# Three pairs of loads become three single loads in a decode block of attention and a bilinear GLU

## The chip, the cores and the metric

The kernel runs on one core of a Trainium2 chip. Its time is the device time of one execution in microseconds (us). Its engines, as the profile names them, are PE (TensorE, with PEld for its weight loads), DVE (VectorE), ACT (ScalarE), POOL (GpSimd) and SP (SyncE, which here issues nearly all transfers). Transfers between the memory of the chip (HBM) and the core's own memory (SBUF) are carried by 16 DMA engines.

## The reference

One token for each of two batch entries goes through a pre-norm attention block with a cache, and then through a bilinear GLU. All data is float32. B = 2, D = 448, 16 heads of 256 values, 8192 cached positions, F = 1792.

```python
q = (x @ wq).reshape(B, Sq, H, Dh).transpose(0, 2, 1, 3)         # x: layernorm of A_x
scores = jnp.einsum("bhqd,bhkd->bhqk", q, k_cache) * (Dh ** -0.5)
p = _softmax(scores, axis=-1)
o = jnp.einsum("bhqk,bhkd->bhqd", p, v_cache)
h = A_x + o.transpose(0, 2, 1, 3).reshape(B, Sq, H * Dh) @ wo

g = jnp.einsum("bsd,df->bsf", _layernorm(h), w_gate)
u = jnp.einsum("bsd,df->bsf", _layernorm(h), w_up)
h2 = h + jnp.einsum("bsf,fd->bsd", g * u, w_down)
```

Each of the 32 pairs of a head and a batch entry, called a query below, has its own 8 MiB of keys and 8 MiB of values. All of the cache is read once: 512 MiB.

## The kernel before

**Tiling.** The 8192 positions of a query are laid out as 128 partitions with 64 positions each; "16 values" or "48 values" below means so many positions on each partition, and 16 of them are 2 MiB. The queries are worked off one after the other (`for n in range(NQ + 1)`, line 550). For a query, VectorE multiplies the keys in place by the query vector and sums over the 256 elements of each position (`scores`, lines 405 to 419). It does this in parts (`score_parts`, line 399): normally 16 values and then 48. Queries 0, 30 and 31, named in `FINE` (line 55), are done in four parts of 16. `top` then takes the largest score, `softmax` the exponentials on ScalarE, and `mix` (line 444) multiplies the probabilities with the values on TensorE: 32 matmuls a query, two positions of each partition in each, 512 columns wide.

**Buffers.** `k_sb` holds 112 values a partition: the keys of even queries lie at values 0 to 63, those of odd ones at 48 to 111, so that two successive queries share 16 values (`OVER`). `v_sb` holds the values of a single query. A load of keys thus waits until VectorE has summed the first 16 values of the query before, and a load of values until `mix` is done with the query before. The values of the last five queries come in pieces, which `LATE` (lines 24 to 30) lists, some of them in parts of the buffers that have come free already.

**Order.** Each engine has a list of its operations in an order written out by hand; the class `Orders` derives the waits from what each operation reads and writes (lines 88 to 113). SP issues all big loads on one queue, in program order, and stops at the first that has to wait. It begins with the weights of the first queries (`d_w0`) and query 0's keys in the pieces of `FIRST` (lines 21 and 262): the last 16 values, the first 16, the middle 32. After that come query 1's keys, query 0's values, query 2's keys, and so on in turn. TensorE runs a loop over the first 27 queries and straight code after that (line 723).

**The end.** The last query's values come in pieces of 16, 32, 8 and 8. `mix` runs over all but the last of them, `open_sums` (line 536) puts the attention result so far and the residual into two accumulators, and `mix` does the last piece. After the values SP loads a last part of `wo`, the gate's weights in two halves, those of "up" in two halves and the down weights in four pieces (lines 605 to 613). The halves divide the columns: F is cut into four groups of 512, 512, 384 and 384 columns, which run on four strips of 32 columns of TensorE; half 0 has the first 256 columns of each group, half 1 the others (256, 256, 128 and 128). `project` (line 618) runs over four row blocks of D, with four matmuls each, one for each group. The operand `xr` is the centred h; its variance is computed by a matmul that stands between the second and the third row block of the gate, and the reciprocal of variance plus epsilon, `rv`, is the scale with which ScalarE copies the gate to `g_sb` (line 675); it does the normalisation of gate and "up" at once. The two halves of "up" follow, each with its product with the gate, two transposes, and then the matmuls of `down` (line 691) as the down weights land.

Of the kernel before, what the change touches and what calls it, by code (L numbers as in the profile page):

```python
# [12 lines left out]
P = 128  # L13
# [3 lines left out]
NJ = SK // P  # L17
HC = 16
OVER = HC

FIRST = ((NJ - HC, NJ), (0, HC), (HC, NJ - HC))


LATE = (
# [1 line left out]
    ((48, None), (16, None)),  # L26
    ((32, None), (32, None)),
    ((32, None), (32, ("k", 0))),
    ((16, ("k", 32)), (32, ("v", 32)), (8, ("v", 0)), (8, ("v", 8))),
)  # L30
WQ, WO = 3 * 2 * DH + DH, 2 * D

FG = (512, 512, 384, 384)
FO = (0, 512, 1024, 1408)
# [1 line left out]
NG = FG[0] // P  # L36

FH = FG[0] // 2
WIDE = [[min(n, (k + 1) * FH) - k * FH for n in FG] for k in range(2)]
PACKED = [3 * sum(n) + n[0] + n[2] for n in WIDE]  # L40

FF = [(n, g) for n in range(4) for g in range(4) if n < FG[g] // P]

# [7 lines left out]
NQ = H * B  # L51
EARLY = NQ - len(LATE)
LOOP = EARLY
DOWN = (5, 5, 3, 1)
FINE = (0, NQ - 2, NQ - 1)


class Orders:
# [135 lines left out]
def decode_block(nc, x, k_cache, v_cache, w, wg, wu, wd, out):  # L194
# [3 lines left out]
    def sb(name, *shape):  # L198
        return nc.alloc_sbuf_tensor(name, list(shape), F32)[:]
# [15 lines left out]
    def mm(out, lhsT, rhs, start, stop, r=(), w=(), mark=None, **kw):  # L215
        put("PE", "matmul", out, lhsT, rhs, start=start, stop=stop, r=r, w=w, mark=mark, **kw)
# [26 lines left out]
    def load_k(i, lo=0, hi=NJ):  # L243
        load_keys(f"d_k_{i}_{lo}", k_cache, i, lo, hi, "k", k_base(i) + lo)
# [13 lines left out]
    def load_w(name, hp, lo, hi, event=None):  # L258
        o.load("SP", name, w_sb[:, lo:hi], w[hp][:, lo:hi], writes=[("w", lo, hi)], event=event)

    load_w("d_w0", 0, 0, WQ)
    for lo, hi in FIRST:
        load_k(0, lo, hi)
# [80 lines left out]
    def q_at(hp, b):  # L344
        k = hp % 2 * B + b
        return qs[k], f"q{k}"

    for k in range(2):
        for b in range(B):
            for c in range(DC):  # L350
                at = c * 2 * DH + (k * DH if c < DC - 1 else 0)
# [5 lines left out]
            got, name = q_at(0, b)  # L357
# [41 lines left out]
    def score_parts(i):  # L399
        at = [(k - 1) % (NJ // HC) * HC if i % 2 == 0 else k * HC for k in range(NJ // HC)]  # L400
        if i in FINE:
            return [(lo, lo + HC) for lo in at]
# [147 lines left out]
    for n in range(NQ + 1):  # L550
        hp, at = divmod(n, 2 * B)
# [49 lines left out]
    k_flat = k_sb.rearrange("p j d -> p (j d)")  # L601
    places = {"wd": 0, "wg": (NJ - OVER) * DH, "wu": (NJ - OVER) * DH + NF * D}
    wd_t, wg_t, wu_t = (k_flat[:, places[n] :][:, : NF * D] for n in ("wd", "wg", "wu"))
    halves = (slice(0, PACKED[0]), slice(PACKED[0], sum(PACKED)))
    for name, t, src in (("wg", wg_t, wg), ("wu", wu_t, wu)):
        for k, half in enumerate(halves):
            o.load("SP", f"d_{name}_{k}", t[:, half], src[:, half],
                   writes=[("k", places[name] + half.start, places[name] + half.stop)])
    at = 0
# [6 lines left out]
        dve("memset", t[2 * 32 :, wide - (FG[0] - FG[2]) : wide], 0.0, w=[name])  # L616

    def project(out, out_name, t, name, k, between=None):
        wide, t = WIDE[k], t[:, halves[k]]
        here = ("k", places[name] + halves[k].start, places[name] + halves[k].stop)  # L620
        for c in range(DC):
            for g in range(4):
                xs = xr[:, c]
                if c < DC - 1:
                    at = c * sum(wide) + sum(wide[:g])
                else:
                    xs = xr[:, c + g % 2]
                    at = 3 * sum(wide) + (wide[0] if g >= 2 else 0)
                mm(
                    out[32 * g : 32 * g + 32, : wide[g]], xs.rearrange("p b r -> p (b r)"),  # L630
                    t[:, at : at + wide[g]], c == 0, c == DC - 1, r=["xr", here], w=[out_name],
                    mark="PE" if c == DC - 1 and g == 3 else None,
                )
            if c == 1 and between is not None:
                between()

    g_ps = q_ps[0]
# [23 lines left out]
        w=["sr"])  # L661
    var = sm[1][:, :1]
    project(
        g_ps[:, :FH], "q_ps0", wg_t, "wg", 0,
        lambda: mm(var, sr.rearrange("p g b r -> p (g b r)"), avg[:, 0:1], True, True,
                   r=["sr", "avg"], w=["sm1"], mark="PE"),
    )
    project(g_ps[:, FH:], "q_ps0", wg_t, "wg", 1)
    oTs = sb("oTs", P, 2, B, 16)
    dve("tensor_copy", oTs, oT[:, :, :, None].to_broadcast([P, 2, B, 16]), r=["oT"], w=["oTs"])  # L670
    last_head(y_ps, "y_ps", oTs.rearrange("p c b r -> p c (b r)"), "oTs", group, False)
# [19 lines left out]
    def down(lo, hi):  # L691
        for k in range(lo, hi):
            n, g = FF[k]
            for q in range(YN):
# [5 lines left out]
                )  # L700

    project(u_ps[0], "q_ps1", wu_t, "wu", 0)
    blank(u_ps[1], "q_ps0", FH)
    project(u_ps[1], "q_ps0", wu_t, "wu", 1, lambda: product(0))
# [36 lines left out]
def pack(np, inputs):  # L741

    got = {n: np.ascontiguousarray(inputs[n]) for n in ("A_x", "A_k_cache", "A_v_cache")}
    wq, wo = np.asarray(inputs["A_wq"]), np.asarray(inputs["A_wo"])
    n = 2 * DH
    rows = []
    for hp in range(H // 2):
        a = wq[:, hp * n : (hp + 1) * n]
        top = a[: 3 * P].reshape(3, P, n).transpose(1, 0, 2).reshape(P, 3 * n)
        last = np.concatenate([a[3 * P :, :DH], a[3 * P :, DH:]], axis=0)  # L750
        rows.append(np.concatenate([top, last], axis=1))

    wo = wo.reshape(H // 2, 2, 2, P, D).transpose(0, 3, 1, 2, 4).reshape(H // 2, P, 2 * WO)
    none = np.zeros_like(wo[:1]), np.zeros_like(rows[0])
    got["w"] = np.concatenate([np.stack(rows + [none[1]]), np.concatenate([none[0], wo])], axis=2)
    for name in ("B_w_gate", "B_w_up"):
        a = np.asarray(inputs[name])
        rows = []
        for k in range(2):
            col = [a[:, FO[g] + k * FH :][:, : WIDE[k][g]] for g in range(4)]  # L760
            top = np.concatenate(col, axis=1)[: 3 * P].reshape(3, P, sum(WIDE[k])).transpose(1, 0, 2)
            last = [np.concatenate([col[q][3 * P :], col[q + 2][3 * P :]], axis=1) for q in range(2)]
            rows += [top.reshape(P, 3 * sum(WIDE[k])), np.concatenate(last, axis=0)]
        got[name] = np.concatenate(rows, axis=1)
    a = np.asarray(inputs["B_w_down"]).reshape(NF, P, D)
    a = a[[FO[g] // P + n for n, g in FF]]
    got["wd"] = a.transpose(1, 0, 2).reshape(P, NF * D)
    return {k: np.ascontiguousarray(v) for k, v in got.items()}
# [27 lines left out]
```

## Time and profile before

| | us |
|---|---|
| median of 3 runs | 1305.08 (1305.04 to 1305.36) |
| the profiled execution | 1305.22 |
| its span, from the first to the last instruction | 1303.9 |
| VectorE busy | 1131.4 (87% of the span) |
| TensorE busy | 489.9 (38%) |
| ScalarE busy | 62.6 (5%) |
| moved by DMA | 561.35 MB, at a mean of 431 GB/s |

Times within the profile count from the start of the span. In rows of the timeline and of the chain, the first number is the start and the second the duration in us; a row ends, in square brackets, with the idle time of the engine ahead of it and what ended it. In rows of DMA issues the last number is the us from the issue to the landing of all of the load; some rows show no size. The row "DMA" of the page cuts the span into 40 equal parts and gives the busy share of the 16 DMA engines in tenths. All operations are recorded by one helper, hence line L207 in nearly all rows, and L154 for the loads; the tiles tell them apart. A float32 matmul shows in the rows as two records.

### The profile page before, as it was taken

Reading aid. Unit: us, or ns where it says so; the run is one execution under the profiler, and the core shown is the slowest. Engines: PE = TensorE matmul, PEld = TensorE weight load, DVE = VectorE, ACT = ScalarE, POOL = GpSimd, SP = SyncE. Lnnn points to the kernel's source line nnn. Section 1 sums busy time; section 2 is a strip of 40 time slices with the busy share of each in tenths; the row PEclk is TensorE's granted clock in tenths of the full one; section 3 lists DMA queues with packets and bytes.
Section 4 is the critical chain, followed back from the end, with each engine's and each line's share of the span. In section 5 each row is a group of like instructions: output and inputs, shape, how many; then the busy total and the mean of one; then the engine's idle time right before and its main releaser. Section 6 shows DMA issues by size and latency. Waiting matters only on the chain.

```text
span 1303.9 us, 6965 instructions
## 1 busy us (share of the span) xinstructions
PE 489.9 (38%) x3004; PEld 170.2 (13%) x3004; DVE 1131.4 (87%) x280; ACT 62.6 (5%) x184; POOL 1.2 (0%) x8
## 2 busy tenths in 40 slices
PE   3035332263321634306343253333424335243267
PEld 2012100020100201102101021100211011011013
DVE  7997998878988789987889878889788897899981
ACT  1000000000000000000000000000000000000000
POOL 0000000000000000000000000000000000000000
PEclk8567655676655867657666576765766667666588
DMA  9999999999999999999999999999999999999998
GB/s 413 436 424 449 420 448 420 440 422 446 420 447 420 442 422 446 422 440 434 432 426 442 438 424 440 426 423 438 450 418 448 414 448 420 447 421 430 434 422 364
DMA packets 13132, 561.35 MB, mean 431 GB/s; under 512 B 1470, under 2 KB 1600, under 8 KB 2112
## 3 DMA queue, kind: packets, MB, share of 16 engines
q1 hardware_dynamic: 13116, 561.19, 99.7%
q8 instruction: 7, 0.11, 0.0%
q14 instruction: 5, 0.04, 0.0%
q10 hardware_dynamic: 4, 0.00, 0.0%
HBM read 561.19 MB, written 0.00 MB: 430 GB/s over the span
## 4 chain that ended last, share of the span: by engine, by line
DMA 71%; DVE 28%; PE 0%; issue 0%; SPq 0%; POOL 0%; ACT 0%; POOLq 0%; DVEq 0%
DMA k_sb<-in_A_k_cache_dram 68%; DVE k_sb L207 14%; DVE s L207 14%; DMA k_sb<-in_wd_dram 3%; DVE nm L207 0%; PE q_ps L207 0%; PE sm L207 0%; DVE xb L207 0%; PE y_ps L207 0%; DVE o_ps L207 0%; SPq L154 0%; POOL ident L207 0%; DVE m L207 0%; ACT q L207 0%; DVE sum_sq_x L207 0%
## 5 line engine op out<-in xcount | busy, mean ns | idle before, releaser
L207 DVE TENSOR_TENSOR k_sb<-k_sb,q 128x4096 f32<-128x4096 f32 x70 | 556.4, 7949 | 134.0 <-DMA k_sb<-in_A_k_cache_dram 130.4
L207 DVE TENSOR_REDUCE s<-k_sb 128x16 f32<-128x4096 f32 x70 | 556.1, 7945 | 0.3
L207 PE MATMUL o_ps<-v_sb,p 128*2 128x512 f32 x2000 | 290.1, 743 | 398.7 <-PEq L161 375.3
L207 PEld LDWEIGHTS o_ps<-v_sb,p 128*2 128x2 f32 x2000 | 53.7, 97 | 606.0 <-issue 578.9
L207 PE MATMUL sm<-nm,row 1*128 1x1 f32 x64 | 16.6, 326 | 194.0 <-PEq L161 170.6
L207 PE MATMUL sm<-ident,m 128*1 128x128 f32 x32 | 10.5, 329 | 139.1 <-PEq L161 99.5
L207 PE MATMUL q_ps<-w_sb,xb 128*128 128x256 f32 (+1 forms) x172 | 60.4, 510 | 0.0
L207 ACT ACTIVATE o_sb<-o_ps 128x512 f32<-128x512 f32 x32 | 19.1, 597 | 689.6 <-PE o_ps L207 689.6
L207 PE MATMUL sm<-sel,o_sb 128*128 128x1 f32 x256 | 33.7, 253 | 25.7 <-PEq L161 22.1
L207 PEld LDWEIGHTS sm<-nm,row 1*128 1x128 f32 x64 | 14.7, 284 | 203.3 <-issue 178.4
L207 PE MATMUL acc_ps<-w_sb,oT 128*2 128x448 f32 x60 | 36.4, 746 | 12.4 <-PEq L161 11.7
L207 PEld LDWEIGHTS sm<-sel,o_sb 128*128 128x128 f32 x256 | 31.8, 195 | 56.4 <-issue 46.5
L207 PEld LDWEIGHTS q_ps<-w_sb,xb 128*128 128x128 f32 x172 | 34.4, 204 | 31.0 <-issue 28.3
L207 PE MATMUL sm<-lsum,ones 128*128 128x1 f32 x64 | 17.3, 339 | 26.0 <-PEq L161 22.3
L207 ACT ACTIVATE nb<-sm 128x1 f32<-128x1 f32 x32 | 5.5, 171 | 411.7 <-PE sm L207 411.7
L207 PEld LDWEIGHTS sm<-ident,m 128*1 128x1 f32 x32 | 2.6, 80 | 150.5 <-issue 107.8
L207 PEld LDWEIGHTS sm<-lsum,ones 128*128 128x128 f32 x64 | 15.3, 298 | 28.0 <-issue 23.9
L207 ACT ACTIVATE q<-q_ps,rstd 128x512 f32<-128x512 f32 (+1 forms) x18 | 11.5, 639 | 73.1 <-PE q_ps L207 73.1
L207 DVE TENSOR_REDUCE total<-o_ps 128x1 f32<-128x128 f32 x1 | 0.3, 291 | 14.1 <-PE o_ps L207 14.1
L207 ACT ACTIVATE p<-s,nb 128x64 f32<-128x64 f32 x32 | 11.1, 348 | 1.0
L207 ACT ACTIVATE oT<-sm,rl 128x2 f32<-128x2 f32 x32 | 8.4, 262 | 39.1 <-PE sm L207 39.1
L207 PE MATMUL q_ps<-k_sb,xr 128*32 128x256 f32 (+1 forms) x128 | 9.9, 425 | 0.9 <-DVE xr L207 0.7
(81 smaller groups left out, 79.0 us busy)
## 6 DMA issues: line engine op xcount, KB each, us to landing
v_sb<-in_A_v_cache_dram SPq DMA_DIRECT2D x4, 4096.0 KB, 30.6
w_sb<-in_w_dram SPq DMA_DIRECT2D x7, 1792.0 KB, 33.6
v_sb<-in_A_v_cache_dram SPq DMA_DIRECT2D x1, 7168.0 KB, 27.3
v_sb<-in_A_v_cache_dram SPq DMA_DIRECT2D x1, 6144.0 KB, 27.6
k_sb<-in_A_k_cache_dram SPq DMA_DIRECT2D x2, 2048.0 KB, 11.3
k_sb<-in_A_k_cache_dram SPq DMA_DIRECT2D x1, 4096.0 KB, 24.2
k_sb<-in_A_v_cache_dram SPq DMA_DIRECT2D x1, 4096.0 KB, 37.7
v_sb<-in_A_v_cache_dram SPq DMA_DIRECT2D x3, 1024.0 KB, 25.2
```

Of the source, the lines that this page charges most:

```text
L207: o.put(engine, lambda: f(*args, **kw), r, w, mark, event)
```

## The change

Query 0's keys come in two loads, the last 16 values and then the other 48, and query 0 leaves `FINE`, so that VectorE works its 48 values in one multiply and one sum, as for most other queries. The last query's last two pieces of 8 values become one of 16; the part of `mix` that follows `open_sums` has then 8 matmuls instead of 4. The gate's weights are packed and loaded as a whole, and the gate has 16 matmuls of 512 or 384 columns instead of 32 of 256 or 128; "up" stays in two halves. SP issues 88 loads of inputs instead of 91, and VectorE has four instructions fewer.

```diff
-FIRST = ((NJ - HC, NJ), (0, HC), (HC, NJ - HC))
+FIRST = ((NJ - HC, NJ), (0, NJ - HC))
...
-    ((16, ("k", 32)), (32, ("v", 32)), (8, ("v", 0)), (8, ("v", 8))),
+    ((16, ("k", 32)), (32, ("v", 32)), (16, ("v", 0))),
...
-WIDE = [[min(n, (k + 1) * FH) - k * FH for n in FG] for k in range(2)]
-PACKED = [3 * sum(n) + n[0] + n[2] for n in WIDE]
+HALVES = [[min(n, (k + 1) * FH) - k * FH for n in FG] for k in range(2)]
+WIDE = {"B_w_gate": [FG], "B_w_up": HALVES}
+
+
+def pieces(name):
+    got, at = [], 0
+    for n in WIDE[name]:
+        to = at + 3 * sum(n) + n[0] + n[2]
+        got.append(slice(at, to))
+        at = to
+    return got
+
+
+PIECES = {"wg": pieces("B_w_gate"), "wu": pieces("B_w_up")}
...
-FINE = (0, NQ - 2, NQ - 1)
+FINE = (NQ - 2, NQ - 1)
...
-    halves = (slice(0, PACKED[0]), slice(PACKED[0], sum(PACKED)))
     for name, t, src in (("wg", wg_t, wg), ("wu", wu_t, wu)):
-        for k, half in enumerate(halves):
+        for k, half in enumerate(PIECES[name]):
...
     project(
-        g_ps[:, :FH], "q_ps0", wg_t, "wg", 0,
+        g_ps, "q_ps0", wg_t, "wg", 0,
         lambda: mm(var, sr.rearrange("p g b r -> p (g b r)"), avg[:, 0:1], True, True,
                    r=["sr", "avg"], w=["sm1"], mark="PE"),
     )
-    project(g_ps[:, FH:], "q_ps0", wg_t, "wg", 1)
```

`project` and the packing of the weights on the host follow the new tables.

More of the change, by code (lines that the diff above doesn't have):

```diff
@@ L618, in project @@
     def project(out, out_name, t, name, k, between=None):
-        wide, t = WIDE[k], t[:, halves[k]]
-        here = ("k", places[name] + halves[k].start, places[name] + halves[k].stop)
+        wide, piece = WIDE[{"wg": "B_w_gate", "wu": "B_w_up"}[name]][k], PIECES[name][k]
+        here = ("k", places[name] + piece.start, places[name] + piece.stop)
+        t = t[:, piece]
         for c in range(DC):
@@ L758, in pack @@
         rows = []
-        for k in range(2):
-            col = [a[:, FO[g] + k * FH :][:, : WIDE[k][g]] for g in range(4)]
-            top = np.concatenate(col, axis=1)[: 3 * P].reshape(3, P, sum(WIDE[k])).transpose(1, 0, 2)
+        for k, wide in enumerate(WIDE[name]):
+            col = [a[:, FO[g] + k * FH :][:, : wide[g]] for g in range(4)]
+            top = np.concatenate(col, axis=1)[: 3 * P].reshape(3, P, sum(wide)).transpose(1, 0, 2)
             last = [np.concatenate([col[q][3 * P :], col[q + 2][3 * P :]], axis=1) for q in range(2)]
-            rows += [top.reshape(P, 3 * sum(WIDE[k])), np.concatenate(last, axis=0)]
+            rows += [top.reshape(P, 3 * sum(wide)), np.concatenate(last, axis=0)]
         got[name] = np.concatenate(rows, axis=1)
```

## The prediction

> **What bounds the kernel now.** I read the page first: the activity of the DMA engines, then the chain that ended last.
>
> ```profile
> DMA  9999999999999999999999999999999999999998
> DMA 71%; DVE 28%; PE 0%; issue 0%; SPq 0%; POOL 0%; ACT 0%; POOLq 0%; DVEq 0%
> ```
>
> The DMA engines are busy in all 40 slices. The chain passes 28% of the span through DVE, so the next question is whether DVE ever leaves the transfer queue empty. The chain in order of time answers it:
>
> ```profile
> 46.86 0.04 DVE m L207
> ...
> 51.60 4.34 DVE s L207
> 55.96 28.46 DMA k_sb<-in_A_k_cache_dram
> ...
> 93.41 34.01 DMA k_sb<-in_A_k_cache_dram
> 127.44 4.43 DVE k_sb L207
> ...
> 166.15 4.43 DVE k_sb L207
> ...
> 1265.83 34.92 DMA k_sb<-in_wd_dram
> ```
>
> A query's keys land 28 to 34 us after their issue, though a query's keys and values (16.78 MB) take only 166.15 - 127.44 = 38.7 us together, thus 433 GB/s and 19.35 us for the keys: each load waits in the queue behind the one before it. The last weights land 34.9 us after their issue. The end is therefore set by the bytes, which the change doesn't alter, as long as (a) the queue never runs dry, (b) the cost that a load adds to the queue stays the same, (c) TensorE still finishes what lands last.
>
> **Part 1, query 0's keys.** Two loads and four VectorE pairs become one load of 48 values and two long instructions. The first fence has the start of the issues (start, us, what), the second the same three loads with their size and us from issue to landing (a size isn't given for a query's whole values), the third VectorE's timeline:
>
> ```profile
> 0.73 0.39 SPq L154 DMA_DIRECT2D w_sb<-in_w_dram  x1
> 2.12 0.63 SPq L154 DMA_DIRECT2D k_sb<-in_A_k_cache_dram  x1
> 20.87 0.43 SPq L154 DMA_DIRECT2D v_sb<-in_A_v_cache_dram  x1
> ```
> ```profile
> w_sb<-in_w_dram SPq DMA_DIRECT2D x1, 896.0 KB, 4.6
> k_sb<-in_A_k_cache_dram SPq DMA_DIRECT2D x1, 4096.0 KB, 24.2
> v_sb<-in_A_v_cache_dram SPq DMA_DIRECT2D x1, 44.2
> ```
> ```profile
> 20.39 4.42 DVE L207 TENSOR_TENSOR k_sb<-k_sb,q 128x4096 f32<-128x4096 f32 x1
> 55.86 12.94 DVE L207 TENSOR_TENSOR k_sb<-k_sb,q 128x12288 f32<-128x12288 f32 x1
> ...
> 81.82 0.22 DVE L207 TENSOR_REDUCE m<-s 128x1 f32<-128x64 f32 x1
> 84.44 4.42 DVE L207 TENSOR_TENSOR k_sb<-k_sb,q 128x4096 f32<-128x4096 f32 x1 [2.40 <-DMA k_sb<-in_A_k_cache_dram]
> ```
>
> The last 32 values land at 2.12 + 24.2 = 26.3; the merged 48 land then too. VectorE, done with the first 16 at about 20.4, stalls until 26.3 (a wait that is new), then runs the two instructions that query 1 shows from 55.86 to 81.82 (26.0 us), to 52.3 where it was 46.86: 5.4 us late. Behind it stand query 1's first 16 values, and for their reduction (51.60, now 57.0) waits the load of query 2's keys, issued at 55.96, now 61.4. What hides this is the value load ahead of it, landing at 20.87 + 44.2 = 65.1. How long before that must the next issue come? The first load, with an empty queue, landed 4.6 us after its issue; its 0.92 MB move in 2.1 us, so 2.5 us are start and landing. Latest issue: 62.6. The cover shrinks from 6.6 to 1.2 us, and holds.
>
> What is late next: VectorE reaches query 2's keys at 82.04 + 5.4 = 87.4, not 84.44, so query 3's keys are issued at 96.4; the load ahead of them lands at 127.42 - 19.35 = 108.1, and the cover is 9 us. A query takes VectorE 35 us (46.86 to 82.04) and 43 lie between 84.44 and 127.44, so the 3 us are gone by then. Query 0's probabilities come 5.4 us later, near 58, before the values that they meet (65.1): the next value load stays at 73.59. Cost: 0. Without the cover it would be 1 us for each us of issue past 62.6.
>
> **Part 2, loads saved.** Three loads fewer. What a queued load adds besides its bytes:
>
> ```profile
> 1251.94 0.33 SPq L154 DMA_DIRECT2D v_sb<-in_A_v_cache_dram  x1
> 1252.31 0.43 SPq L154 DMA_DIRECT2D v_sb<-in_A_v_cache_dram  x1
> 1254.26 0.91 SPq L154 DMA_DIRECT2D k_sb<-in_B_w_gate_dram  x2
> ```
> ```profile
> v_sb<-in_A_v_cache_dram SPq DMA_DIRECT2D x1, 1024.0 KB, 23.1
> v_sb<-in_A_v_cache_dram SPq DMA_DIRECT2D x1, 1024.0 KB, 25.2
> k_sb<-in_B_w_gate_dram SPq DMA_DIRECT2D x1, 1792.0 KB, 28.7
> k_sb<-in_B_w_gate_dram SPq DMA_DIRECT2D x1, 1344.0 KB, 31.4
> ```
>
> The two loads of 8 values land at 1275.04 and 1277.51: 2.47 us for 1.05 MB, which 433 GB/s move in 2.42. The gate's second part comes at 1254.74 + 31.4 = 1286.1, 3.2 us after the first, for 1.38 MB (3.17). A load adds about 0.06 us, from 0 to 0.15 by the rounding of these rows. Three: -0.2 us, bounds 0 and -0.45. SP saves three issues of 0.43, worth nothing: it is 28 us ahead there. The merged gate load needs the keys of part 2 free (VectorE is past them at 1251), so its issue isn't delayed.
>
> The Trainium skill ("DMA: Bandwidth & Descriptors", Bandwidth) says that a transfer of 1 MB reaches 78% of peak at 6.15 us, and advises batches of at least that; by it each of the 8-value loads would cost 3.7 us more than its bytes, and the sum, as an estimate, would be 11 us lower. The 2.47 us above do not agree: that page's time is of a transfer by itself.
>
> **Part 3, the tail.** The last 16 values land at 1277.5 as the second 8 did. TensorE runs 16 matmuls, the residual sums, then 8, instead of 20, the sums, then 4: its order changes, not its work, so the part ends as before. The gate is different:
>
> ```profile
> 1285.30 1.93 PE L207 MATMUL q_ps<-k_sb,xr 128*32 128x256 f32 x16 [0.67 <-DVE xr L207]
> 1291.57 0.69 ACT L207 ACTIVATE g_sb<-q_ps,rv 128x512 f32<-128x512 f32 x1 [7.84 <-PE q_ps L207]
> 1293.83 1.06 PE L207 MATMUL q_ps<-k_sb,xr 128*32 128x256 f32 x16 [0.23 <-DMA k_sb<-in_B_w_up_dram]
> 1299.18 1.17 PE L207 MATMUL y_ps<-k_sb,hmT 128*32 128x112 f32 x40 [0.93 <-DMA k_sb<-in_wd_dram]
> ```
> ```profile
> 1285.30:1289.40 4.10, 3.65 (x34) 1.39 (x38) 0.00 (x0) 0.00 (x0) 0.50 0.99 416
> 1289.40:1291.60 2.20, 2.14 (x38) 1.22 (x32) 0.00 (x0) 0.03 (x1) 0.91 0.99 415
> ```
>
> The first fence is the timeline, the second TensorE's work on the gate by stretches (PE busy, with records, then PEld, DVE, ACT; granted clock, DMA share, GB/s). Before, the gate started at 1285.30, when its operand xr was ready; now it needs all its weights, 1286.0: 0.7 us late. A 256-column record took 3.65/34 = 0.107 us at clock 0.50 and 0.056 at 0.91; 512 columns twice that. The first two row blocks (16 records) end at 1289.5, the variance (0.5) at 1290.0, the other 16 records, with the clock back as before, at 1291.8. ScalarE's g_sb comes 0.3 us late. Bounds: 1291.4 (half of the records have only 384 columns) and 1293.4 (half clock throughout, 1.9 late). Cover: 0.23 us before the second half of "up" and 0.93 before the down weights. So 0.3 costs nothing, 1.9 would cost some 0.7. I take 0, since the row of the stretch from 1289.40 shows the clock coming back after four busy us.
>
> The Trainium skill ("TensorE: Matmul & The Clock Gate", What's actually happening) puts the return of the clock after one busy window of about 3.4 us, with a free phase; the 0.50 and then 0.91 above agree, and by the latest phase, 6.8 us after 1286.0, the sum would be the upper bound, +0.7.
>
> **Sum.** 0 - 0.2 + 0 = -0.2 us against the profiled execution's 1305.22, that is 1305.0. The median of the runs lies 0.14 lower: 1304.9.
>
> **Rivals.**
>
> A. Slower: the clock stays at half to the end, as the wait for the whole gate lengthens TensorE's idle stretch ahead of it.
>
> ```profile
> 1291.60:1301.80 10.20, 8.22 (x190) 1.00 0.79 323
> ```
>
> This row is all of TensorE's work after the gate (busy, records, clock): 8.22 us at full clock. From the gate's end at 1293.4, twice that (16.4) and 0.6 for hand-overs end at 1310.4, not 1301.8: 8.6 us, 1313.7. Over 0.2% only if the clock comes back after about 1297 (0.3 late, half a us for each us past 1290, 1.2 of cover). Against it: TensorE works without a gap from 1286.0 as before from 1285.30, where the clock came back.
>
> B. Slower: the queue runs dry at 65 us. From an issue at 62.6 on, 1 us each; over 0.2% from 65.4, that is 9.4 us late and not 5.4. For 8 us late it costs 1.4 (1306.3), for 10 us 3.4 (1308.3). For it: only 1.2 us are left; against: the lengths are all from rows.
>
> C. Faster: each load pays the 2.5 us of the first by itself; three fewer give 1305.08 - 7.5 = 1297.6. The 2.47 us of a queued load speak against it. The Trainium skill's rule under part 2 would work in this way.
>
> D. Another lag, either sign:
>
> ```profile
> q8 instruction: 1, 0.02, 1.6%
> ```
>
> Query 0's keys are all there at 26.3, where 9.31 MB from 0.73 on need 2.5 + 21.5, that is 24.7: 1.6 us of lag, which 19.35 us a load never make up. Between 21 and 25 us the DMA engines passed one packet of the instruction queue (packets, MB, share). If instruction code is fetched elsewhere among the 16 engines, that lag goes (1303.3) or comes twice (1306.5); no row shows which engine it is.
>
> **How the numbers follow.** About 0.2% (2.6 us) is what a measurement of this kernel can tell from no change. Forecast, with a tail late by up to 0.7: 0.70. D: 0.12. A: 0.07. B beyond 0.2%: 0.06. C: 0.05. Within 0.2%: 0.70 + 0.12 = 0.82; slower 0.13; faster 0.05. The range is 1303.3 to 1306.6, which takes in the forecast and both ends of D; A, B beyond it and C (0.18) are left out.
>
> **What would show it.** VectorE waits near 5.9 us on the DMA before query 0's second multiply and ends it near 52; query 2's keys are issued near 61.4 and land near 84.4; query 3's land near 127.4. The last values land at 1277.4, the gate starts at 1286, g_sb near 1291.8, and the last wait is again for the last down weights. Wrong, if query 2's keys land after 85, if the last wait is TensorE's own, or if the clock reads 0.50 after 1293.

## The result, and the profile after

The changed kernel takes 1307.12 us (median of 22 runs, 1305.32 to 1307.94), the kernel before 1305.07 (22 runs, 1304.83 to 1305.87). The ratio is 1.0015, with a 95% interval of 1.0009 to 1.0021: slower by 2.05 us, within the 0.2% named in the prediction, but outside its range and on the other side of the forecast. The runs also lie 2.6 us apart, where those of before lie 1.0 apart.

The profiled execution took 1305.76 us, span 1304.1, and is the second shortest of the 22. It shows nearly what was predicted. Its chain and VectorE's timeline at the start, the issue of query 2's keys, and their landing (us after the issue):

```profile
52.22 0.04 DVE m L219
...
87.39 4.33 DVE k_sb L219
...
96.27 31.02 DMA k_sb<-in_A_k_cache_dram
127.31 4.43 DVE k_sb L219
```
```profile
26.24 12.96 DVE L219 TENSOR_TENSOR k_sb<-k_sb,q 128x12288 f32<-128x12288 f32 x1 [5.35 <-DMA k_sb<-in_A_k_cache_dram]
```
```profile
61.31 0.33 SPq L166 DMA_DIRECT2D k_sb<-in_A_k_cache_dram  x1
```
```profile
k_sb<-in_A_k_cache_dram SPq DMA_DIRECT2D x1, 23.0
```

VectorE waits for the 48 values until 26.2, is done with query 0 at 52.2, and query 2's keys are issued at 61.3 and landed at 84.3, as in the kernel before. The end, from the chain and the timeline:

```profile
1266.22 34.75 DMA k_sb<-in_wd_dram
1300.97 0.04 issue
1301.02 1.02 PE y_ps L219 x32
```
```profile
1286.56 3.63 PE L219 MATMUL q_ps<-k_sb,xr 128*32 128x512 f32 x16 [0.96 <-DMA k_sb<-in_B_w_gate_dram]
1292.94 0.69 ACT L219 ACTIVATE g_sb<-q_ps,rv 128x512 f32<-128x512 f32 x1 [8.24 <-PE q_ps L219]
1299.42 1.17 PE L219 MATMUL y_ps<-k_sb,hmT 128*32 128x112 f32 x40 [0.77 <-DMA k_sb<-in_wd_dram]
```

The gate waits 0.96 us for its weights, g_sb comes 1.4 us later than before, and TensorE still waits 0.77 us (0.93 before) for the down weights. So this profile doesn't show where the 2 us go. They arise in the slower executions, of which it is not one.

### The profile page after: what moved, and what is told of

It is laid out like the page before. It is cut to its first block, busy times and chain, and to the rows that moved or that the text cites. A ratio compares the mean times of both kernels' runs of the same rounds, so it can differ in the third digit from the quotient of the medians.

```text
span 1304.1 us, 6894 instructions
## 1 busy us (share of the span) xinstructions
PE 493.6 (38%) x2972; PEld 170.3 (13%) x2972; DVE 1131.0 (87%) x276; ACT 62.6 (5%) x184; POOL 1.3 (0%) x8
## 4 chain that ended last, share of the span: by engine, by line
DMA 70%; DVE 29%; issue 0%; SPq 0%; PE 0%
DMA k_sb<-in_A_k_cache_dram 67%; DVE k_sb L219 14%; DVE s L219 14%; DMA k_sb<-in_wd_dram 3%; DVE nm L219 0%; SPq L166 0%; PE y_ps L219 0%; DVE m L219 0%; DVE y L219 0%; DVE rl L219 0%
## 5 line engine op out<-in xcount | busy, mean ns | idle before, releaser
L219 PE MATMUL sm<-sel,o_sb 128*128 128x1 f32 x256 | 34.5, 256 | 25.7 <-PEq L173 22.1
L219 PE MATMUL o_ps<-k_sb,p 128*2 128x512 f32 x48 | 10.0, 994 | 4.7 <-DMA k_sb<-in_A_v_cache_dram 4.7
```

Of the source, the lines that this page charges most:

```text
L219: o.put(engine, lambda: f(*args, **kw), r, w, mark, event)
```

## Which of the three merges costs it

Two theories. Start theory: rival B, the transfer queue runs dry near 65 us in most executions. Tail theory: the later gate, or the later last values, use up TensorE's cover at some phases of its clock. Each merge was run alone, and the changed kernel once more.

**Query 0's keys alone:**

```diff
-FIRST = ((NJ - HC, NJ), (0, HC), (HC, NJ - HC))
+FIRST = ((NJ - HC, NJ), (0, NJ - HC))
-FINE = (0, NQ - 2, NQ - 1)
+FINE = (NQ - 2, NQ - 1)
```

> Only query 0's keys are merged (16 and 48). If the transfer queue runs dry near 65 us in most executions (start theory), this alone costs about the whole 2 us: some 1307, with the spread of the changed kernel. If the cost is in the tail (gate or values theory), it costs nothing: 1304.9 to 1305.2, all runs within 1 us, and query 2's keys land near 84.3.

Measured: 1307.16 us (1306.0 to 1307.68), ratio 1.0015 (1.0006 to 1.0024); the kernel before on this chip 1305.17. The whole loss is here.

**The last values alone:**

```diff
-    ((16, ("k", 32)), (32, ("v", 32)), (8, ("v", 0)), (8, ("v", 8))),
+    ((16, ("k", 32)), (32, ("v", 32)), (16, ("v", 0))),
```

> Only the last two pieces of 8 values are merged. Values theory: the last piece now leaves 8 matmuls instead of 4 behind the residual sums, so the last softmax-weighted sum and all that follows come up to 1 us later and the cover of 1.2 us in front of the last down weights is gone in some phases of TensorE's clock: 1305.5 to 1306. Gate theory and start theory: 1305.0, as before.

Measured: 1305.08 us (1304.91 to 1305.5), ratio 1.0001 (0.9992 to 1.001). No cost.

**The gate alone** (the changed kernel with query 0's loads and the last values as before):

```diff
-WIDE = [[min(n, (k + 1) * FH) - k * FH for n in FG] for k in range(2)]
+HALVES = [[min(n, (k + 1) * FH) - k * FH for n in FG] for k in range(2)]
+WIDE = {"B_w_gate": [FG], "B_w_up": HALVES}
```

> Only the gate's weights are merged (512 columns a matmul). Gate theory: the gate starts near 1286 and not 1285.3, and its half-clock part is 3.4 us and more; in the phases of the clock that bring the full clock late, TensorE ends after the last weights have landed: 1306 to 1307, with a spread of 2 us or more. Start theory and values theory: 1305.0 with a spread under 1 us.

Measured: 1305.2 us (1304.88 to 1305.66), ratio 1.0 (0.9991 to 1.0009). No cost and no spread: the tail theory falls.

**All of it again:**

> The changed kernel as it is, for its time on the same chip as its parts and for a second profile. About 1307, 1305.3 to 1308. Any tail theory: a profile of a slower execution ends with TensorE waiting for itself and not for the down weights, at another phase of the clock. Start theory: query 2's keys land later than 84.4 there, and all later landings with them.

Measured: 1306.9 us (1306.67 to 1307.65), ratio 1.0014 (1.0005 to 1.0023). This time the profiled execution took 1307.13 us, and it shows where the time goes. Its issue and landing of query 2's keys, and its chain:

```profile
61.33 0.33 SPq L166 DMA_DIRECT2D k_sb<-in_A_k_cache_dram  x1
```
```profile
k_sb<-in_A_k_cache_dram SPq DMA_DIRECT2D x1, 23.8
```
```profile
96.28 31.82 DMA k_sb<-in_A_k_cache_dram
128.12 4.42 DVE k_sb L219
137.09 30.44 DMA k_sb<-in_A_k_cache_dram
...
851.63 30.68 DMA k_sb<-in_A_k_cache_dram
...
1302.66 0.04 issue
```

The same rows of the kernel before:

```profile
136.41 29.72 DMA k_sb<-in_A_k_cache_dram
...
850.21 30.02 DMA k_sb<-in_A_k_cache_dram
```

The keys were issued at the same 61.3 as in the execution of 1305.76 us, but landed at 85.1, 0.7 us after the 84.4 of before. Two later loads take 0.7 us longer each (30.44 for 29.72, 30.68 for 30.02). With the 0.2 us that part 2 estimated for three loads saved that is 0.7 + 0.7 + 0.7 - 0.2 = 1.9 us, and the last down weights land at 1302.66 for 1300.75, 1.9 us later. These rows put the loss at three places, and only the first is that of rival B. They show the slowest DMA engine alone, though. In the execution of 1305.76 us the place near 850 us costs 0.3 us over before as well:

```profile
850.10 30.30 DMA k_sb<-in_A_k_cache_dram
```

## Why it comes in steps: sixteen engines, one landing time

The row of a load has one landing time, that of its slowest DMA engine. The trace also holds the completions of each of the 16, and their packets. The table is worked out from them. "Idle" is the mean time from 62 to 68 us in which an engine had no packet of data. "Longer" is what packets of 64 KB that began from 62 to 72 us took beyond their usual 2.42 us, added up, per engine. Then follow the first, the 15th and the last completion of query 0's values, and the mean and the last of the 16 for query 2's keys and for the last load. The two lower rows are runs of the next section.

```
                           issue  idle longer   values: 1st  15th   last   keys 2: mean  last   end: mean    last
before (1305.22 us)        55.96  0.00  0.00          62.93 63.55  65.07          82.74 84.42     1300.02 1301.30
after (1305.76)            61.31  0.00  0.05          63.28 64.21  64.92          83.13 84.28     1300.33 1301.53
query 0's keys (1306.47)   61.41  0.40  0.49          62.94 63.65  65.06          83.50 84.44     1301.12 1302.50
all again (1307.13)        61.33  0.63  0.92          62.90 63.60  64.96          84.19 85.10     1301.32 1303.19
late scores (1308.38)      61.62  0.30  0.79          62.94 63.71  65.16          83.82 86.04     1301.18 1304.45
8 us late (1308.20)        63.76  1.91  0.75          63.07 63.76  65.02          85.33 85.90     1302.65 1304.16
```

The cover that the prediction counted, up to 65.1, was that of a single engine. It lags by 1.5 us, and the lag begins where a packet of instruction code goes by at 22 us (rival D): in the kernel before, the slowest engine is 0.3 us behind the mean of the 16 in a load that lands at 15 us, and 1.7 in the one at 25. The other 15 have landed all of theirs by 62.9 to 63.6. In the executions of 1306.47 and 1307.13 us at least 7 of them then stand idle until the keys of query 2 reach them, 1.9 to 3.3 us after the issue. The packets that follow are longer too, up to 3.5 us instead of 2.42. Idle time and longer packets together are 0.89 and 1.55 us; from the mean completion of the values to that of the keys the two executions take 0.80 and 1.51 us more than the 19.35 of before. So more than half of what the average engine loses there is not idle time, but longer packets. Why they are longer stays open.

In the execution of 1305.76 us each engine went on at once, at the same issue time. In that one the first packets of query 1's keys, near 24 us, had already been longer, and the engines ran out 0.35 us later on average. That the issue was in time there for this reason is a reading of one trace; if so, it was luck.

The average engine loses hardly more after this. At the end of "all again" its last load is 1.30 us later than before, where query 2's keys were 1.45 later; in "query 0's keys" it is 1.10 for 0.76. The rest lies in how far the slowest engine is behind the mean: at the end 1.28 us before, 1.38 and 1.87 in these two. In the kernel before, 15 engines were 1.5 us ahead of the one that lagged, and most of what held one of them up later was hidden by that; of the places above, the one near 850 us costs 0.3 us there (30.02 for 29.72). Now they have lost much of that lead. In both kernels a packet of the instruction queue goes by near 137 or 111 us and near 850; the row of the execution "all again" from 130 to 147 us (packets, MB, share):

```profile
q14 instruction: 1, 0.01, 0.1%
```

On the engine that it passed, the next data packet took 3.03 us instead of 2.42. In the execution of 1305.76 us the same packet at 137 us costs the end nothing: its load takes 29.72 us. In "query 0's keys" even the landing of query 2's keys tells nothing (84.44 for 84.42), while the end is 1.2 us later: the time was lost on engines ahead of the slowest. That the packets meet these engines is read from the trace; no run put one elsewhere.

The Trainium skill ("DMA: Bandwidth & Descriptors", Why a DMA increments its semaphore by 16 and not by 1) says that a transfer runs on up to 16 engines that finish independently, with the semaphore counting them. The completions of query 0's values, from 62.90 to 64.96 in "all again", agree.

## Late issue or large load

Is it VectorE's lateness that costs, or the load of 48 KB a partition? The changed kernel has both. **The loads of before, with the late scores:**

```diff
-FINE = (0, NQ - 2, NQ - 1)
+FINE = (NQ - 2, NQ - 1)
```

> The loads of the kernel before (16, 16 and 32 values), but VectorE takes query 0's 48 values in one multiply and one sum, for which it waits for all of them. Late-issue theory (VectorE's lateness of 5.4 us brings query 2's keys to the queue after most DMA engines have run dry): 1306.5 to 1307.3, like the merged load. Load theory (the single load of 48 KB a partition is what costs): 1305.1.

Measured: 1306.25 us (1305.63 to 1308.53), ratio 1.001 (1.0001 to 1.0019). VectorE's timeline:

```profile
26.54 12.96 DVE L207 TENSOR_TENSOR k_sb<-k_sb,q 128x12288 f32<-128x12288 f32 x1 [6.07 <-DMA k_sb<-in_A_k_cache_dram]
```

With the loads untouched and only VectorE late, the loss and the spread are there. The profiled execution is one of the two slowest, at 1308.38 us. Its issue and landing of query 2's keys:

```profile
61.62 0.33 SPq L154 DMA_DIRECT2D k_sb<-in_A_k_cache_dram  x1
```
```profile
k_sb<-in_A_k_cache_dram SPq DMA_DIRECT2D x1, 24.4
```

They land at 86.0, since one engine got its first packet 3.9 us after the issue. The average engine loses 1.1 us up to there, between the two delayed executions above; but at the end one engine is 3.3 us behind the mean (2.5 behind the next), and the time is 3.2 us over that of before. The run's median is 0.25 us under the band expected; whether the large load adds a part, or this other chip has its own share of undelayed executions, stays open.

**Lateness by itself.** The kernel before, with a sum of constants on VectorE ahead of query 1's scores, once of 3 us and once of 8 (`k` is 22 and 58):

```diff
+    junk = sb("junk", P, k)
     late = None
     for n in range(NQ + 1):
+        if n == 1:
+            dve("tensor_reduce", junk, ones[:, None, :].to_broadcast([P, k, P]), axis=AX.X,
+                op=ALU.add, r=["ones"], w=["junk"])
```

> The kernel before, with a sum of constants that holds VectorE for 3 us after query 0's scores (its result is used by nothing). Late-issue theory: query 2's keys are issued near 59.0, start within 3.3 us of that, and no engine is free before 62.4: 1305.2. Load theory: 1305.2 too.

> The same with 8 us. Late-issue theory: query 2's keys are issued near 64.0, and 15 of the 16 DMA engines, free from 62.4 to 63.2 on, stand idle for 2 to 4 us each: 1308 to 1309.5. Load theory: 1305.2, as the loads are those of before.

Measured: 1305.15 us (1304.95 to 1305.4), ratio 1.0 (0.9991 to 1.0009), for 3 us; 1307.89 (1307.52 to 1308.28), ratio 1.002 (1.0011 to 1.0029), for 8. The issue of query 2's keys in the first and in the second, VectorE's added work in the second, and the landing there:

```profile
58.95 0.33 SPq L154 DMA_DIRECT2D k_sb<-in_A_k_cache_dram  x1
```
```profile
47.01 7.88 DVE L207 TENSOR_REDUCE junk<-ones 128x58 f32<-128x7424 f32 x1
```
```profile
63.76 0.33 SPq L154 DMA_DIRECT2D k_sb<-in_A_k_cache_dram  x1
```
```profile
k_sb<-in_A_k_cache_dram SPq DMA_DIRECT2D x1, 22.1
```

Issued at 58.95, nothing runs dry (idle 0.00 by the same reckoning) and nothing is lost. Issued at 63.76, all 16 engines stand idle, 1.9 us on average, and lose 0.75 us more in longer packets; the median is 2.7 us over that of before, a little under the 1308 expected. The last landing alone (63.76 + 22.1 = 85.9, 1.5 us later than before) again shows half of it: the mean completion of these keys is 2.6 us later (85.33 for 82.74). The spread is small here (0.8 us); no engine could go on at once. Between the two doses lies the edge. The changed kernel's 61.3 is at it, and that explains its spread as far as the executions of 1305.76 and 1307.13 us show it.

**The cover given back.** The changed kernel, with one load of weights moved ahead of query 2's keys, for n = 1 alone:

```diff
+        if n == 1:
+            load_w("d_w_1", 1, 0, WQ + 2 * WO, event("e_w", n))
         if n + 1 < NQ:
             load_k(n + 1)
         for part in parts[1:]:
             load_v(n - 1, part)
-        if at == 1:
+        if at == 1 and n > 1:
```

> The changed kernel, with the weights of the next heads (1.8 MB, 4.3 us of transfer) issued ahead of query 2's keys instead of behind them, once, so that the queue holds 4.3 us more when those keys are issued near 61.3. Late-issue theory: nothing runs dry, 1304.8 to 1305.2 with all executions within 1 us. Load theory: 1307 as before this edit.

Measured: 1304.92 us (1304.86 to 1305.55), ratio to before 0.9998 (0.9989 to 1.0008). Issue and landing:

```profile
61.73 0.33 SPq L166 DMA_DIRECT2D k_sb<-in_A_k_cache_dram  x1
```
```profile
k_sb<-in_A_k_cache_dram SPq DMA_DIRECT2D x1, 27.3
```

VectorE is as late and the 48 values come in one load, but the keys now queue behind 4.3 us of weights: idle 0.00, and both the loss and the spread are gone. All three merges together then stand 0.24 us under the kernel before in the medians (1305.16 on that chip), close to the 0.2 us of part 2; the interval doesn't tell that from no change.

## Why the prediction was wrong, point by point

- **What bounds the kernel.** Right: the bytes, as long as the queue doesn't run dry. Condition (a) is the one that broke.
- **Part 1, the times.** Right within 0.1 us in the profiled execution: the stall ends at 26.2 (26.3 predicted), query 0 ends at 52.2 (52.3), the keys are issued at 61.3 (61.4), query 3's land at 127.3.
- **Part 1, the cover.** This step failed: "Latest issue: 62.6. The cover shrinks from 6.6 to 1.2 us, and holds." It was counted from the landing row of query 0's values (65.1), which is the last of 16 engines. By the prediction's own 2.5 us for start and landing, the 15 others, done by 62.9 to 63.6, need the issue by 60.4 to 61.1. It came at 61.3: by this estimate no cover was left, -0.2 to -0.9 us. Rival D held the clue, a lag of 1.6 us that began near 22 us; it is the lag of one engine, and the rest were that much earlier.
- **Part 1, "Cost: 0".** Measured: 2.0 us (1307.16 against 1305.17). Nor does "1 us for each us of issue past 62.6" fit: issued at 63.76, which that puts at 1.2 us, the keys cost 2.7, of which 1.9 are idle time and 0.75 the longer packets, for which the prediction had no term.
- **Part 2.** -0.2 us: the medians fit it (the merges with the cover given back: -0.24), but no run separates it from zero.
- **Part 3.** Right in the result, with sizes off: the gate began at 1286.56 (1286.0), and its row names the weights as what came last; its operand was late too, since the last values were summed 1 us later (o_sb at 1281.30 against 1280.32). g_sb came at 1292.94 (1291.8). "Its order changes, not its work, so the part ends as before" was thus 1 us off, and the granted clock was 0.50 up to 1290.6 and 0.85 on average from there to 1292.9. The cover held all the same: values and gate alone cost nothing.
- **Rivals.** B named the place and the mechanism, but its price starts at least 1.3 us too late (62.6, where 61.3 already costs 2 us), and its chance of 0.06 was for a cost beyond 0.2% only; a cost of 2 us had none of its own and lay outside the range. D took the lag as something that goes or comes twice; in the kernel before it mattered as what the other engines were ahead by. A (a clock that stays at half) and C (each load's own 2.5 us) didn't occur: the 2 us are explained without them, the last wait was again for the down weights, and two loads fewer in the tail gained nothing that can be seen.
- **What would show it.** "Wrong, if query 2's keys land after 85" was the right sign in the execution of 1307.13 us (85.1) and not in that of "query 0's keys" (84.44), where the slowest engine's landing doesn't show the loss.

## What to carry to other kernels

When an edit makes a transfer's issue later, count its cover from the time when the first DMA engine runs out of data, not from the landing of the load ahead: a landing is that of the slowest of sixteen engines, and the others may be 2 us ahead. A queue that runs dry on some engines need not move the next landing at all; the average of the sixteen has moved all the same, and the lost lead comes due later, when something small holds one of them up. An issue at the edge shows as a spread of the runs, so a single profile, which may be of an undelayed execution, can look harmless; giving back a few us of queued transfer ahead of the late issue is a cheap test and here the cure.

## What the runs showed of the hardware that was not expected

- The time from a load's issue to an engine's first packet differs between engines and executions. With all engines idle (8 us late) it was 0.95 to 1.9 us; with engines just running out it was 1.1 to 3.3 us in "all again" and up to 3.9 in "late scores", although the issue was the same instruction. Why engines that ran out a little earlier or later were served so late stays open. (The packed trace gives a packet no engine; packets whose end and start meet were taken as one engine's.)
- After the queue had run dry on some engines, 15 to 24 packets of 64 KB took 2.6 to 3.5 us instead of 2.42, which cost the average engine 0.5 to 0.9 us. Where nothing ran dry (before, 3 us late, the cover given back) none did in this stretch; in the execution of 1305.76 us three did, the longest 2.75.
- The slowest engine fell 1.5 us behind the others where a packet of instruction code of 16 KB went by at 22 us, and in the kernel before it is still 1.6 us behind the mean at 840 us. A packet of 8 KB costs its engine 0.9 us (0.31 for itself, 0.6 for the data packet behind it).
- 0.4 to 0.6 us of idle time of the average DMA engine went with 1.3 to 2 us at the end of the execution (1306.47 and 1307.13 against 1305.17): the longer packets add 0.5 and 0.9 us, and the slowest engine ends 0.1 and 0.6 us further behind the mean than before.
